# One ScalarE side operation instead of two at the end of each of the first twenty units

## Chip, cores and metric

The kernel runs on one core of one Trainium2 chip. The metric is the device time of one execution in microseconds (us). It is given as the median of several runs, and one further execution was recorded by the hardware profiler. Engines are named as in the profile: PE (TensorE matmul), PEld (its weight loads), DVE (VectorE), ACT (ScalarE), POOL (GpSimd), SP (SyncE, which here issues every DMA).

## Reference

Three layers run one after the other, all in float32.

```
# 1. mLSTM, 4 batches x 8 heads, 768 steps, head size 40
m_new = max(f + m, i);  fs = exp(f + m - m_new);  is_ = exp(i - m_new)
C = fs*C + is_ * outer(v_t, k_t);  n = fs*n + is_*k_t
y_t = sigmoid(o_gate_t) * (C q_t) / max(|n.q_t|, 1)
# 2. soft mixture of experts, 3072 tokens x 320, 8 experts x 4 slots, FF 1024
logits = x @ phi;  d = softmax over tokens;  c = softmax over slots
out = c @ [ relu((d.T @ x)_e @ w1[e]) @ w2[e] for e ]
# 3. MLP: relu(x @ w_in)**2 @ w_out,   320 -> 2048 -> 320
```

## Kernel before

**The units.** The first layer is cut into 11 groups of up to three heads and six chunks of 128 steps: 66 units (u0 to u65). Each turn of the loop over `units` (L881) issues the parts of several units. It makes the gate broadcast of unit i+3 (`e_mb`, L440), the scores of unit i+2 (`e_st`, L471), the state update of unit i (`e_u`, L499, then `e_uc`, L518 or L515, then the masking `e_mask` on POOL, L534), the product of scores and gate weights of unit i+2 (`e_pm`, L483 on DVE), the exponentials of unit i+3 (`e_exp`, L454, three on ACT), and their triangle mask (`e_sel`, L461 on POOL). Every second unit multiplies the weights with the values (`e_av`, L559) and the queries with the state before (`e_inter`, L544).

**The side work.** Everything else of this stage stands in a list `fillers` of generators, each of which yields the tag of its next step: "A" for a step on ACT, "n" and "N" for DVE, "D" for DVE, "G" and "g" for POOL, "P" for PE, "W" for a point to wait for or a DMA to issue. `advance(tag, limit)` runs up to `limit` steps whose tag is asked for; `filler(seq)` calls it for each letter of `seq`. At the end of each unit `filler(END, ...)` runs with END = "PADNngG". The "A" steps are the gate's tanh (`sigm`, L660, 12 in all), the absolute values in `fin` (L607), copies and exponentials of the expert layer (`moe_tokens`), and the conversions of `w_in` (`win_all`, which calls `narrow`).

**The conversion of w_in.** `win_all` loads ten pieces of `w_in` (128x1024 words, L168) in turn into the two halves of the tile `stage`, and converts each in four steps: L140 and L144 on ACT, L148 and L152 on DVE. A piece's load waits until the conversion that read its half is done. The generator is always sorted to the end of `fillers`. Its "n" steps run only where the unit has run no other "N" or "D" step. When all ten are converted, "win" stands in `done`, and only then the first two halves of the expert layer's second weight (w2 of f = 0) are loaded into the same tile:

```
        if "win" in done and w2s:
            ld_w2(*w2s.pop(0))
...
    while fillers:
        advance("W")
        filler("PNADngG")
    while w2s:
        ld_w2(*w2s.pop(0))
```

The first two lines stand in the loop over units, the others behind it. Behind them follow, on the same SP queue, the w2 halves of f = 3 into `par0` (`ld_w2`, L123; in the kernel before they are part of one run of three), `wo0` (the first four row blocks of `w_out`, L991), two half-size loads of `w_out` (`xTw`, `x`), w2 of f = 4 (`w2x`) and w2 of f = 5 to 7 (six halves into `ring`, over the first weights, which L1113 must have read). SP issues in program order, so a DMA that waits holds all behind it.

**The expert layer's end.** `ffn_up` (L1113) multiplies the slots with w1; `relu` (L1118 on ACT) needs `rt128` (L1137 on DVE). Ahead of L1137 on DVE stand L148 and L152 of `wo_narrow(0)`, which convert `wo0`, behind L140 and L144 of the same on ACT. `ffn_tr` (L1164) transposes the result, and `ffn_down(f)` (L1183, f = 0 to 7) multiplies it with w2 of f, two halves each. The last layer (L1226 on) follows.

Of the kernel before, what the change touches and what calls it, by code (L numbers as in the profile page):

```python
# [18 lines left out]
PL, DL, SG = 2, 2, 2  # L19
# [4 lines left out]
LI, LT = 42, "NADG"  # L24
# [18 lines left out]
def kernel(  # L43
# [20 lines left out]
    D = DM // H  # L64
# [746 lines left out]
    def split(t):  # L811
        return (t, set()) if not isinstance(t, tuple) else t
# [6 lines left out]
    def advance(tag, limit=9):  # L819
        n = limit  # L820
        for f in list(fillers):
            while limit and f[1] in tag and f[3] <= done:
                limit -= 1
                t = next(f[0], None)
                if t is None:
                    fillers.remove(f)
                    done.add(f[2])
                    break
                f[1], f[3] = split(t)
        return n - limit  # L830
# [9 lines left out]
    def filler(seq, late=False, early=False):  # L840
        nn = 0
        for ch in seq:
            if ch == "n":
                if not nn:
                    advance("n", DL)
                continue
            k = advance(ch, {"P": PL, "A": 2, "D": 2 - early, "G": 2 - early}.get(ch, 1) + (late and ch in LT))
            nn += k if ch in "ND" else 0

    w2o = [(f, p) for f in range(FF // 128) for p in range(2)]  # L850
# [28 lines left out]
    late = []  # L879
    xq = [(b, c) for b in range(1, B) for c in range(0, NC, 2)]  # L880
    for i, (g, c) in enumerate(units):  # L881
# [41 lines left out]
        if MID:  # L923
            filler(MID)
# [36 lines left out]
        if i + 3 < NU:  # L961
# [3 lines left out]
            elif g3 > 1 and c3 % 3 == 0:  # L965
                e_wv(g3, c3, c3 + 3)
        filler(END, i >= LI, i < 20)
    xf = xb[B - 2].rearrange("p c d -> p (c d)")
    hsb = xf[:, 0:FF]
# [8 lines left out]
# [3 lines that stand above are left out]
# [525 lines left out]
```

## Time and profile before

| | us |
|---|---|
| median of 3 runs | 390.84 (390.78 to 390.98) |
| the profiled execution, its own time | 390.83 |
| its span, first to last instruction | 389.1 |
| PE busy | 379.6 |
| DVE busy | 264.5 |
| ACT busy | 253.4 |
| POOL busy | 102.4 |

The span is what the trace's times count in, from 0 to 389.1; 1.7 us of the execution's own time lie outside it. The units run from about 10 to 153 us, the end of the expert layer from there to about 182, the last layer from there to the end. A start time in a timeline row is that of the first instruction of the row; where it has "x24", 24 instructions are merged. An idle time in brackets stands ahead of the row's first instruction, with what ended it.

### The profile page before, as it was taken

What the parts mean: (1) busy time and instruction counts of PE and PEld (TensorE: products, weight loads), DVE (VectorE), ACT (ScalarE), POOL (GpSimd) and SP (SyncE); (2) the same over time, 40 slices, a digit from 0 to 9 for tenths busy, and PEclk for the clock granted to TensorE, in tenths of its full rate; (3) what the DMA queues carried; (4) which work ended last, traced back from release to release, by engine and by line L of the source; (5) the groups of instructions that cost most, each with busy time, mean ns of one, the idle gap of its engine ahead of it and who ended that gap; (6) DMA issues with size and microseconds to landing.
All of it is one profiled execution on the core that took longest, in us unless ns stands there. A gap on an engine that the chain in (4) does not pass through costs nothing.

```text
span 389.1 us, 9201 instructions
## 1 busy us (share of the span) xinstructions
PE 379.6 (98%) x3438; PEld 335.1 (86%) x3438; DVE 264.5 (68%) x614; ACT 253.4 (65%) x579; POOL 102.4 (26%) x208
## 2 busy tenths in 40 slices
PE   8899899999999999999999999999999999999996
PEld 6799798798988885435799999999999999999996
DVE  7978788777878777537699956556555655655551
ACT  7797754768566653344697976676676667667662
POOL 4665867775667645000000000000000000000000
PEclk9999999999999999999999999999999999999999
DMA  6886987898879896999000010020010001002001
GB/s 194 257 297 208 289 275 232 254 332 286 260 255 338 286 320 201 361 374 374 3 2 1 3 67 2 0 69 0 3 60 10 0 2 67 3 0 69 1 2 67
DMA packets 19541, 56.62 MB, mean 146 GB/s; under 512 B 2481, under 2 KB 7561, under 8 KB 19113
## 3 DMA queue, kind: packets, MB, share of 16 engines
q1 hardware_dynamic: 19497, 56.04, 42.6%
q8 instruction: 27, 0.44, 0.5%
q14 instruction: 17, 0.14, 0.1%
HBM read 52.10 MB, written 3.93 MB: 144 GB/s over the span
## 4 chain that ended last, share of the span: by engine, by line
PE 84%; ACT 5%; DVE 4%; DMA 2%; issue 2%; POOL 1%; SPq 0%; DVEq 0%; ACTq 0%; POOLq 0%
PE ps_mb L1404 17%; PE ps_st L1404 16%; PE ps_st L471 9%; PE ps_lt L1404 9%; PE ps_o L559 5%; PE ps_o L544 4%; PE ps_o L1327 4%; PE ps_mb L499 3%; PE ps_st L1183 2%; PE ps_mb L440 2%; ACT w L454 2%; PE ps_m L1327 2%; PE ps_lt L683 2%; PE ps_m L677 2%; DMA par<-in_q_t_dram 1%
## 5 line engine op out<-in xcount | busy, mean ns | idle before, releaser
L1350 DVE CAST hi<-ring 128x512 fp32r<-128x512 f32 x93 | 39.7, 427 | 59.1 <-ACT ring L1349 49.7
L454 ACT ACTIVATE w<-ps_mb,qt 128x128 f32<-128x128 f32 x192 | 56.7, 371 | 29.6 <-DVE cu L518 23.4
L1351 DVE TENSOR_TENSOR lo<-ring,hi 128x512 fp32r<-128x512 f32 x96 | 66.5, 693 | 10.1 <-PE ps_o L1327 0.5
L1332 ACT ACTIVATE ring<-ps_o 128x512 f32<-128x512 f32 x65 | 38.9, 598 | 35.0 <-PE ps_o L1327 35.0
L1349 ACT ACTIVATE ring<-ring 128x512 f32<-128x512 f32 x93 | 58.8, 632 | 3.0
L471 PE MATMUL ps_st<-par 120*128 120x128 f32 (+1 forms) x384 | 56.9, 284 | 0.4 <-DMA par<-in_q_t_dram 0.4
L1404 PE MATMUL ps_mb<-wohlh,hi 128*128 128x320 f32 x160 | 49.6, 311 | 0.0
L1404 PE MATMUL ps_mb<-wohlh,lo 128*128 128x320 f32 x160 | 49.5, 310 | 0.0
L1404 PE MATMUL ps_mb<-wohll,hi 128*128 128x320 f32 x160 | 49.3, 309 | 0.0
L471 PEld LDWEIGHTS ps_st<-par 120*128 120x128 f32 (+1 forms) x384 | 47.9, 191 | 0.8 <-DVE dec L415 0.5
L461 POOL TENSOR_SCALAR_AFFINE_SELECT w<-w 128x384 f32<-128x384 f32 (+1 forms) x66 | 37.3, 567 | 38.1 <-ACT w L454 37.2
L1404 PE MATMUL ps_st<-wohlh,hi 128*128 128x320 f32 x144 | 44.8, 311 | 0.0
L483 DVE TENSOR_TENSOR p<-ps_st,w 128x384 f32<-128x384 f32 (+1 forms) x66 | 35.7, 540 | 13.4 <-POOL w L461 7.0
L1404 PE MATMUL ps_st<-wohll,hi 128*128 128x320 f32 x144 | 44.7, 310 | 0.0
L1404 PE MATMUL ps_st<-wohlh,lo 128*128 128x320 f32 x144 | 44.7, 310 | 0.0
L1404 PEld LDWEIGHTS ps_mb<-wohll,hi 128*128 128x128 f32 x160 | 30.1, 188 | 1.3
L1332 ACT ACTIVATE ring<-ps_m 128x512 f32<-128x512 f32 x31 | 18.5, 598 | 18.4 <-PE ps_m L1327 18.4
L1404 PEld LDWEIGHTS ps_mb<-wohlh,hi 128*128 128x128 f32 x160 | 30.0, 188 | 0.0
L1404 PEld LDWEIGHTS ps_mb<-wohlh,lo 128*128 128x128 f32 x160 | 30.0, 188 | 0.0
L559 PE MATMUL ps_o<-par,p 128*64 128x41 f32 x768 | 29.0, 232 | 0.0
L1404 PEld LDWEIGHTS ps_st<-wohll,hi 128*128 128x128 f32 x144 | 27.1, 188 | 1.9 <-issue 0.6
L559 PEld LDWEIGHTS ps_o<-par,p 128*64 128x64 f32 x768 | 25.1, 137 | 4.0 <-issue 0.2
(277 smaller groups left out, 777.8 us busy)
## 6 DMA issues: line engine op xcount, KB each, us to landing
ring<-in_w_dram SPq DMA_DIRECT2D x22, 640.0 KB
stage<-in_w_in_dram SPq DMA_DIRECT2D x10, 512.0 KB
par<-in_w_dram SPq DMA_DIRECT2D x6, 640.0 KB
out_dram<-ring SPq DMA_DIRECT2D x24, 160.0 KB
par<-in_v_s_dram SPq DMA_DIRECT2D x9, 369.0 KB
par<-in_k_s_dram SPq DMA_DIRECT2D x9, 360.0 KB
x<-in_o_gate_dram SPq DMA_DIRECT2D x9, 320.0 KB
par<-in_k_t_dram SPq DMA_DIRECT2D x23, 120.0 KB
```

Of the source, the lines that this page charges most:

```text
L454: nc.scalar.activation(w[:, j, :], mb[:, 128 * j : 128 * j + 128], AF.Exp, bias=qt3[:, c, h0 + j : h0 + j + 1])
L461: nc.gpsimd.affine_select(out=w, in_=w, pattern=[[0, nh], [1, 128]], compare_op=ALU.is_ge, fill=0.0, base=0, channel_multiplier=-1)
L471: nc.tensor.matmul(st[:, 128 * j : 128 * j + 128], lhsT=kbd[g % 2][0:nd, j, ts_], rhs=qin[g][0:nd, ts_], start=True, stop=True,)
L483: nc.vector.tensor_tensor(out=p, in0=sts.pop((g, c))[:, 0 : nh * 128].rearrange("p (n t) -> p n t", n=nh), in1=ws.pop((g, c)), op=ALU.mult,)
L544: nc.tensor.matmul(pos[g, c // 2][:, o0 : o0 + nv], lhsT=qin[g][0:nd, 128 * c : 128 * c + 128], rhs=cbds[g, c - 1][0:nd], start=True, stop ...
L559: nc.tensor.matmul(po[t0 : t0 + 64, o0 : o0 + DV], lhsT=p[:, j, t0 : t0 + 64], rhs=vin[g][:, c, j, :], start=True, stop=True,)
L1327: nc.tensor.matmul(t, lhsT=gst[n][:, 128 * k : 128 * k + 128], rhs=cst[tg], start=True, stop=True)
L1332: nc.scalar.activation(r, t, AF.Relu)
L1349: nc.scalar.activation(r, r, AF.Square)
L1350: nc.vector.tensor_copy(hi, r)
L1351: eng.tensor_tensor(out=lo, in0=r, in1=hi.bitcast(F32), op=ALU.subtract)
L1404: nc.tensor.matmul(acc[u][:, 0:DM], lhsT=l_[:, 128 * u : 128 * u + 128], rhs=wohl[r_, f // 8][:, f % 8, :], start=(f == 0 and a == 0), sto ...
```

## Change

At the end of a unit the letter "A" ran up to two steps on ACT. Now it runs up to two only from the twentieth unit on; until then up to one, as "D" and "G" already did (`early` is true for i < 20).

```diff
-            k = advance(ch, {"P": PL, "A": 2, "D": 2 - early, "G": 2 - early}.get(ch, 1) + (late and ch in LT))
+            k = advance(ch, {"P": PL, "A": 2 - early, "D": 2 - early, "G": 2 - early}.get(ch, 1) + (late and ch in LT))
```

What that does to the order is seen on three engines. The number of instructions on each is the same, PE and POOL keep their order, and from u17 to u54 the conversions stand where they stood, two pieces later in count.

On ACT, at u12 to u16 (L660 the tanh, L454 the units' exponentials, L607 the absolute values, L140 and L144 the conversion of `w_in`), the kernel before has:

```order
L454 ACTIVATE w<-ps_mb,qt_109 128x128 x3
L660 ACTIVATE x<-x 128x640
L454 ACTIVATE w<-ps_mb,qt_109 128x128 x3
L607 ACTIVATE rc<-ring 128x18
L140 ACTIVATE wi<-stage 128x512
L454 ACTIVATE w<-ps_mb,qt_109 128x128 x3
L144 ACTIVATE stage<-stage 128x512
L454 ACTIVATE w<-ps_mb,qt_109 128x128 x3
L607 ACTIVATE rc<-ring 128x18
L454 ACTIVATE w<-ps_mb,qt_109 128x128 x3
```

The changed kernel has there:

```order
L454 ACTIVATE w<-ps_mb,qt_109 128x128 x3
L660 ACTIVATE x<-x 128x640
L454 ACTIVATE w<-ps_mb,qt_109 128x128 x3
L607 ACTIVATE rc<-ring 128x18
L454 ACTIVATE w<-ps_mb,qt_109 128x128 x3
L144 ACTIVATE stage<-stage 128x512
L454 ACTIVATE w<-ps_mb,qt_109 128x128 x3
L607 ACTIVATE rc<-ring 128x18
L454 ACTIVATE w<-ps_mb,qt_109 128x128 x3
```

The L140 of u14 is gone, and the L144 of u15 belongs to the first piece instead of the third. In u8 to u12 the kernel before has two more L140 and two L144, the changed one has a single L140 at u10. The two pieces that are done later on ACT stand at u56 and u57, and at u62 and u64.

On DVE, behind the last unit (L652 and L653 end the first layer, L1034 opens the last token block's softmax), the difference is:

```order
 L652 RECIPROCAL rcl<-rcl 128x4
 L653 TENSOR_TENSOR x<-x,rcl 128x2x80
+L148 SCALAR_TENSOR_TENSOR stage<-stage 128x512
+L152 SCALAR_TENSOR_TENSOR wi<-wi,stage 128x512
 L1034 TENSOR_REDUCE nmx<-ps_lt 96x1
 L1036 TENSOR_SCALAR mx_114<-nmx 96x1
```

The tenth piece's conversion ends there; before, it stood at u54, and the ninth's, now at u60, stood at u50.

On SP, at the end of the units, the difference is:

```order
 L116 DMA ring<-in_w_dram 128x1280
-L123 DMA par_70<-in_w_dram 128x1280 x3
+L123 DMA par_70<-in_w_dram 128x1280
+L123 DMA stage<-in_w_dram 128x1280 x2
+L123 DMA par_70<-in_w_dram 128x1280 x2
 L991 DMA wo_2724<-in_w_out_dram 128x2560
 L991 DMA xTw<-in_w_out_dram 128x1280
```

The two w2 loads into `stage` moved here, ahead of two of the three loads into `par0` and of `wo0`. Before, they were issued in the units around u54. Two loads of `w_in` pieces (L168) moved from u12 and u15 to u50 and u54.

## Rows read from the trace of the kernel before

**Rows 1.** Busy time of each engine by stretch: length, engines, PEclk, DMA share, GB/s.

```profile
30.00:40.00 10.00, 10.00 (x141) 9.45 (x141) 7.66 (x18) 8.21 (x23) 5.39 (x11) 1.00 0.67 197
```

**Rows 2.** Timeline of PE in u9 to u15.

```profile
30.94 0.89 PE L471 MATMUL ps_st<-par 120*128 120x128 f32 x6
...
34.40 0.89 PE L471 MATMUL ps_st<-par 120*128 120x128 f32 x6
...
42.34 0.48 PE L544 MATMUL ps_o<-cbd,par 120*128 120x123 f32 x2 [1.21 <-POOL cbd L534]
```

**Rows 3.** Timeline of ACT and POOL ahead of that wait.

```profile
38.14 0.66 ACT L140 ACTIVATE wi<-stage 128x512 f32<-128x512 f32 x1
...
38.71 0.86 ACT L454 ACTIVATE w<-ps_mb,qt 128x128 f32<-128x128 f32 x3
...
39.65 0.53 POOL L461 TENSOR_SCALAR_AFFINE_SELECT w<-w 128x384 f32<-128x384 f32 x1 [1.02 <-ACT w L454]
...
41.45 0.84 POOL L534 TENSOR_TENSOR cbd<-cu,hm 120x123 f32<-120x123 f32 x1
```

**Rows 4.** Instructions that touch `stage`: ns min/median/max, first and last start.

```profile
L140 ACT ACTIVATE wi<-stage x10: 662/679/723, 26.2 to 120.9; 128x512 f32<-128x512 f32 x10
L144 ACT ACTIVATE stage<-stage x10: 662/702/728, 28.1 to 122.3; 128x512 int32<-128x512 uint16 x10
L148 DVE SCALAR_TENSOR_TENSOR stage<-stage x10: 672/810/1129, 29.3 to 126.5; 128x512 int32<-128x512 int32 x10
L152 DVE SCALAR_TENSOR_TENSOR wi<-wi,stage x10: 691/888/1178, 30.0 to 127.2; 128x512 int32<-128x512 int32 x10
```

**Rows 5.** Timeline of DVE behind the last unit.

```profile
154.80 0.33 DVE L653 TENSOR_TENSOR x<-x,rcl 128x160 f32<-128x160 f32 x1
156.90 0.42 DVE L1034 TENSOR_REDUCE nmx<-ps_lt 96x1 f32<-96x256 f32 x1 [1.77 <-PE ps_lt L1021]
```

**Rows 6.** Timeline of SP: the issue of loads.

```profile
127.25 0.35 SPq L123 DMA_DIRECT2D stage<-in_w_dram  x1
...
149.31 4.02 SPq L123 DMA_DIRECT2D par<-in_w_dram  x3
155.29 0.33 SPq L991 DMA_DIRECT2D wo<-in_w_out_dram  x1
```

**Rows 7.** DMA issues from 145 to 190 us: count and KB each.

```profile
ring<-in_w_dram SPq DMA_DIRECT2D x6, 640.0 KB
...
wo<-in_w_out_dram SPq DMA_DIRECT2D x1, 1280.0 KB
```

**Rows 8.** Busy time by stretch at the end of the expert layer.

```profile
150.00:156.00 6.00, 5.80 (x60) 3.60 (x56) 3.96 (x17) 1.72 (x5) 2.07 (x6) 1.00 0.93 309
158.00:182.00 24.00, 23.92 (x257) 10.24 (x258) 14.15 (x41) 10.53 (x19) 1.90 (x2) 1.00 1.00 389
168.00:182.00 14.00, 14.00 (x177) 5.80 (x166) 9.03 (x19) 7.65 (x14) 0.00 (x0) 1.00 1.01 409
```

**Rows 9.** Timeline of ACT and DVE around the first `relu`.

```profile
160.88 0.78 ACT L140 ACTIVATE par<-wo 128x640 f32<-128x640 f32 x1 [0.31 <-DMA wo<-in_w_out_dram]
...
167.39 0.69 ACT L1118 ACTIVATE x<-ps_st,rt 128x512 f32<-128x512 f32 x1 [5.06 <-DVE rt L1137]
167.98 0.80 ACT L140 ACTIVATE par<-wo 128x640 f32<-128x640 f32 x1
...
167.20 0.16 DVE L1137 COPY rt<-ps_m 128x1 f32<-128x1 f32 x1 [1.07 <-PE ps_m L1136]
...
171.13 0.35 DVE L1049 COPY en<-ps_o 128x192 f32<-128x192 f32 x1
```

**Rows 10.** Timeline of PE: the first transposes, the last halves of w2, what follows.

```profile
170.12 0.66 PE L1164 MATMUL ps_mb<-ident,x 128*128 128x128 f32 x4
...
178.56 3.41 PE L1183 MATMUL ps_st<-ring 128*32 128x320 f32 x48
181.90 0.66 PE L1226 MATMUL ps_m<-ident,chl 128*128 128x128 f32 x4
```

## Prediction

> **What bounds the kernel now.** I read the engine totals first: PE is busy for 379.6 of the 389.1 us, so time is won only where PE really waits, and lost wherever a change makes it wait. The busy time by stretch then says where the change could help: from 30 to 40 us ACT is busy for 8.21 of 10 us [rows 1], the densest it gets beside the tanh steps, so that taking ACT work out looks promising there. But PE is busy for all 10. A busy PE can be an illusion of modelled ends, so the next view is PE's timeline by start times. Two units repeat one pattern, and the scores of every second unit start at 30.94 and 34.40 [rows 2], 3.46 us apart, with no idle time marked between them. PE is the pace there, and ACT's density is hidden under it. The first wait of PE behind this stretch is at 42.34: 1.21 us for the masked state from POOL [rows 2]. That is the one place where less ACT work can give something back.
>
> The third view is the end of the units and of the expert layer, since the change moves work there. From 158 to 182 us the DMA engines are busy for 100% of the time at a mean of 389 GB/s, and from 168 to 182 at 409 GB/s [rows 8]. PE is busy too (23.92 of 24 us), so today loads and PE just keep step. A load that comes later into this stretch pushes all behind it.
>
> **The change part by part.**
>
> *Early.* Four ACT steps (two L140, two L144) and four DVE steps (two L148, two L152) leave u8 to u15. By the medians [rows 4] that is 2 x (0.68 + 0.70) = 2.8 us of ACT and 2 x (0.81 + 0.89) = 3.4 us of DVE. Up to about 41 us they are worth nothing: PE sets the pace over them (3.46 us for two units). The cover is gone at 42.34. The chain into that wait runs: L140 at 38.14 holds the exponentials to 38.71, POOL's mask L461 at 39.65 had waited 1.02 us for them, and two more POOL operations stand between it and the state's masking L534 at 41.45 [rows 3], which PE waits for. The changed order has no L140 there, so the exponentials and all behind them come 38.71 - 38.14 = 0.57 us earlier. L148 and L152 of u15 stay where they are, only with another piece. Bounds: nothing (if POOL is held by something else) to the whole wait of 1.21 us. I take -0.6, since the removed L140 is directly ahead of the chain and the rest of POOL's queue does not change.
>
> *Middle.* From u17 to u54 each step stands where it stood. 0.
>
> *Late.* Two pieces are converted in u56 to u64 and behind the units. Two pairs of ACT steps go in, 2.8 us by the same medians, and one DVE pair at u60, 1.7 us. ACT and DVE have idle time between units there, and what waits for the exponentials (POOL, then L483 on DVE, one unit later) has a unit's time. Bounds: 0 to 1.0 us, the latter if one of the pairs falls fully on the way; I take +0.1. The last DVE pair stands between L653, which ends at 154.80 + 0.33 = 155.13, and L1034, which had been idle for 1.77 us until PE at 156.90 [rows 5]. The shortest L148 and L152 take 0.67 + 0.69 = 1.4 us, the medians 1.7 [rows 4]: both fit under that wait, 0. If the cover failed, the longest (1.13 + 1.18) would cost 0.5.
>
> *The w2 loads into `stage`.* They were issued from 127.25 on [rows 6] and had landed long before use. Now the first waits for the last L148, so SP issues it at about 155.13 + 0.7 = 155.9. SP is in program order, so two of the `par0` loads (issued from 149.31 on before) and `wo0` (155.29 before) come behind it [rows 6]. The queue between 153 and 156 us runs dry, and from 155.9 on it has to bring: stage 2, par0 2, `wo0` 1280 KB which is 2, the two half loads of w_out 1 each, w2x 2, and ring 6 halves of 640 KB [rows 7]; all halves of w2 are the same shape. That is 16 x 655,360 bytes = 10.49 MB up to the last half of f = 7, and 6 halves = 3.93 MB up to `wo0`.
>
> How fast: 409 GB/s, as in the stretch where the queue is never short [rows 8]; the 389 of the longer stretch has two short dips in it and is the lower bound. How long until a fresh queue moves: from 149.31 to 156 it brought 6 x 309 = 1.85 MB [rows 8], which at 409 takes 4.5 us, so the start-up is at most about 2 us (part of it is SP's own spacing); at least 0. I take 2, the only row that has it. Then `wo0` lands at 155.9 + 2.0 + 9.6 = 167.5 (160.88 before, [rows 9]) and the last half of w2 at 155.9 + 2.0 + 25.6 = 183.5.
>
> What waits: L140 of `wo0` on ACT, and through L144, L148, L152 the L1137 on DVE. The second such conversion shows the length of that chain: L140 at 167.98, and the next DVE instruction behind its L152 (L1049) at 171.13, so 3.15 us [rows 9]. L1137 comes at 167.5 + 3.15 = 170.65 instead of 167.20, the relu L1118 starts 0.19 later (as 167.39 to 167.20) and takes 0.69 [rows 9]. PE's first transposes L1164 then start at about 171.5 instead of 170.12 [rows 10]: +1.4. All of f = 0 to 7 moves by that. The 48 instructions of f = 5 to 7 take from 178.56 to 181.90 [rows 10], so the last half (8 of them) starts at 181.34, and 1.4 later at 182.7. But it lands at 183.5: another 0.8 us. The end of the expert layer moves by 1.4 + 0.8 = 2.2 us, and since nothing behind it waits for a fixed time, the kernel's end does too. Bounds: with no start-up, `wo0` at 165.5 is still in time and the last half at 181.5 costs 0.2; with 389 GB/s and 2 us the last half lands at 184.9: 3.5.
>
> A rule of the Trainium skill bears on the rate: "DMA: Bandwidth & Descriptors", section "Bandwidth", says that for loads from HBM the HBM share of a core, about 358 GB/s, is what binds. By that figure the last half would land (an estimate) at 187.2 and the tail would cost 5.9 us. The 409 GB/s held over 14 us in [rows 8] contradict it for this run, and the measured figure decides.
>
> *Sum.* Against the profiled execution's own 390.83 us (span 389.1 and 1.7 around it; the median of the runs, 390.84, is the same): 390.83 - 0.6 + 0.1 + 2.2 = 392.5 us.
>
> **The rivals.** A change under 0.2% (0.8 us) cannot be told from none.
> - *The loads are hidden anyway* (no change). If the queue starts at once and runs at 409, the tail costs 0.2: 390.83 - 0.6 + 0.1 + 0.2 = 390.5. For it: no PE wait on a load shows in this stretch today, so some slack exists (the last half, by the same sum, had landed at 160.88 + 10 x 0.655 / 0.409 = 176.9 against 181.34). Against it: 1.31 MB more in a queue that is 100% busy take 3.2 us, and the dry time ahead takes the rest.
> - *The early relief wins* (faster). The whole wait at 42.34 goes, -1.2, and the tail costs the 0.2 above: 389.8. It decides from the point where the tail costs less than about 0.4, that is if `wo0` lands before 166. For it: ACT's removed step is right ahead of the chain. Against it: the DVE pair of u15, beside which POOL's L534 took 0.84 us [rows 3], is still there, and the tail has to be nearly free.
> - *Both late costs come* (slower still). 389 GB/s and a late pair on the way, with no early gain: 390.83 + 1.0 + 3.5 = 395.3. For it: the mean over the longer stretch. Against it: its dips come where the queue ran short, which a backlog does not.
> - That the change does nothing is excluded: the order of ACT, DVE and SP changes as shown.
>
> **How the numbers follow.** The forecast, a tail of 1 to 3.5 us and a small early gain, gets 0.67; hidden loads 0.17; the early relief 0.08; both late costs 0.08. The predicted time is 392.5; the likeliest case's own range is 391.7 to 394.0. The range for 8 in 10 reaches from the hidden loads to the upper bound of the tail without the early gain, 390.4 to 394.3, and leaves out the faster case and the slowest. Chances: faster 0.08, the same 0.17, slower 0.75.
>
> **What would show it right or wrong.** Right: SP issues the two w2 loads into `stage` at about 155 to 156 (shifted by the early gain) instead of 127; almost no DMA between 153 and 156; ACT's L140 of `wo0` waits for its DMA until 167; L1118 about 3.5 us later; PE's L1164 waits; and the halves of f = 6 and 7 have PE waits on the `ring` loads. The stretch u9 to u14 keeps its 3.46 us per two units, and the wait at 42.34 is halved. Wrong: a queue that brings `wo0` by 165, or a pace of units that drops under 3.46 us without the conversions, or new PE waits at u56 to u62, which I cost at 0.1.

## Result and profile after

The changed kernel takes 393.98 us in the median (393.58 to 395.18, 4 runs) against 390.91 us of the kernel before beside it: a ratio of 1.0084 (95% interval 1.0071 to 1.0096), 3.1 us slower. The profiled execution took 393.82 us with a span of 392.1, that is 3.0 us more than before in both. The direction was as forecast, and so was the chain of waits at the end; of the two terms that make the sum, the early gain was 1.55 us instead of 0.6, by a second path, and the loss at the end 4.5 us instead of 2.2.

**Early.** PE's timeline of the changed kernel at the place of [rows 2] (start, duration, line, form; idle time in brackets):

```profile
30.88 0.89 PE L471 MATMUL ps_st<-par 120*128 120x128 f32 x6
...
34.34 0.89 PE L471 MATMUL ps_st<-par 120*128 120x128 f32 x6
...
40.15 0.89 PE L471 MATMUL ps_st<-par 120*128 120x128 f32 x6
40.92 0.48 PE L544 MATMUL ps_o<-cbd,par 120*128 120x123 f32 x2
```

The pace of 3.46 us for two units has not changed, and the wait of 1.21 us ahead of L544 is gone altogether. What stands ahead of it on DVE, ACT and POOL, in the same profile:

```profile
35.91 0.40 DVE L588 TENSOR_TENSOR ring<-ps_o,tmp 128x246 f32<-128x246 f32 x1
...
36.35 0.23 ACT L607 ACTIVATE rc<-ring 128x18 f32<-128x18 f32 x1 [0.20 <-DVE ring L588]
37.27 0.88 ACT L454 ACTIVATE w<-ps_mb,qt 128x128 f32<-128x128 f32 x3 [0.69 <-DVE cbd L515]
...
38.23 0.53 POOL L461 TENSOR_SCALAR_AFFINE_SELECT w<-w 128x384 f32<-128x384 f32 x1 [1.21 <-ACT w L454]
...
40.03 0.84 POOL L534 TENSOR_TENSOR cbd<-cu,hm 120x123 f32<-120x123 f32 x1
```

Against [rows 3] the exponentials come 1.44 us earlier (37.27 against 38.71) and L534 1.42 us earlier. ACT has even become idle ahead of them: the step L140 that was removed had 0.57 us, so something else moved too. It is L607, which in the kernel before started at 38.00 and had itself waited for DVE's L588; and L588 stood behind the pair L148, L152 of u12, which the change also removed. In the kernel before:

```profile
35.42 0.84 DVE L148 SCALAR_TENSOR_TENSOR stage<-stage 128x512 int32<-128x512 int32 x1
36.29 0.89 DVE L152 SCALAR_TENSOR_TENSOR wi<-wi,stage 128x512 int32<-128x512 int32 x1
...
37.57 0.40 DVE L588 TENSOR_TENSOR ring<-ps_o,tmp 128x246 f32<-128x246 f32 x1
...
38.00 0.23 ACT L607 ACTIVATE rc<-ring 128x18 f32<-128x18 f32 x1 [0.63 <-DVE ring L588]
```

With the pair gone, L588 comes 1.66 us earlier and L607 1.65. By u23 the units run 1.55 us earlier, and they keep that to the last one: the late conversions cost nothing.

**Late.** SP's issue of loads (compare [rows 6]), with the time that issuing took as the second column:

```profile
147.76 0.33 SPq L123 DMA_DIRECT2D par<-in_w_dram  x1
154.24 1.02 SPq L123 DMA_DIRECT2D stage<-in_w_dram  x2
155.35 1.07 SPq L123 DMA_DIRECT2D par<-in_w_dram  x2
156.52 0.50 SPq L991 DMA_DIRECT2D wo<-in_w_out_dram  x1
```

Then ACT, DVE and PE around the first `relu` (compare [rows 9, 10]):

```profile
167.41 0.82 ACT L140 ACTIVATE par<-wo 128x640 f32<-128x640 f32 x1 [8.40 <-DMA wo<-in_w_out_dram]
...
170.73 0.69 ACT L1118 ACTIVATE x<-ps_st,rt 128x512 f32<-128x512 f32 x1 [1.82 <-DVE rt L1137]
...
155.35 0.42 DVE L1034 TENSOR_REDUCE nmx<-ps_lt 96x1 f32<-96x256 f32 x1 [0.45 <-PE ps_lt L1021]
...
171.47 0.89 PE L1164 MATMUL ps_mb<-ident,x 128*128 128x128 f32 x4 [2.84 <-ACT x L1118]
172.29 3.32 PE L1113 MATMUL ps_o<-ring,x 128*32 128x512 f32 x16
175.44 1.25 PE L1183 MATMUL ps_st<-stage,ring 128*32 128x320 f32 x16
...
181.54 3.41 PE L1183 MATMUL ps_st<-ring 128*32 128x320 f32 x48
184.89 0.66 PE L1226 MATMUL ps_m<-ident,chl 128*128 128x128 f32 x4
```

SP waits for the last conversion from 148.1 to 154.24; `wo0` is released only 13.1 us behind the first load into `stage`; L1118 and PE wait for it, PE by 2.84 us. Last, the busy time by stretch (length, engines, PEclk, DMA share, GB/s):

```profile
152.00:154.00 2.00, 2.00 (x16) 1.23 (x14) 1.90 (x8) 0.26 (x2) 0.98 (x2) 1.00 0.01 4
...
156.00:168.00 12.00, 11.62 (x101) 4.95 (x104) 3.52 (x20) 1.76 (x6) 1.90 (x2) 1.00 1.00 404
168.00:182.00 14.00, 11.16 (x120) 4.44 (x116) 7.86 (x15) 7.96 (x15) 0.00 (x0) 0.88 1.02 416
...
171.80:175.20 3.40, 3.40 (x20) 0.96 (x21) 2.30 (x5) 1.12 (x3) 0.00 (x0) 0.50 1.01 411
```

The queue is empty from 152 to 154, then full at 404 and 416 GB/s, so the rate was the 409 of the forecast to within 2%. Behind PE's wait its granted clock is at 0.50, the lower of its two levels (1.2 instead of 2.4 GHz), for 3.4 us. From L653, the end of the units, to L1226, the first matmuls of the last layer, it takes 31.64 us instead of 27.10: 4.54 more, less the 1.55 won, is the 3.0 of the span.

### The profile page after: what moved, and what is told of

Read it like the earlier page. It is cut to its first block, busy times and chain, and to the rows that moved or that the text cites. A ratio compares the mean times of both kernels' runs of the same rounds, so it can differ in the third digit from the quotient of the medians.

```text
span 392.1 us, 9201 instructions
## 1 busy us (share of the span) xinstructions
PE 380.5 (97%) x3438; PEld 335.1 (85%) x3438; DVE 264.7 (68%) x614; ACT 253.2 (65%) x579; POOL 102.8 (26%) x208
## 4 chain that ended last, share of the span: by engine, by line
PE 84%; ACT 5%; DVE 4%; DMA 3%; issue 1%; POOL 1%; SPq 0%; ACTq 0%; DVEq 0%; POOLq 0%
PE ps_mb L1404 17%; PE ps_st L1404 16%; PE ps_st L471 10%; PE ps_lt L1404 8%; PE ps_o L559 6%; PE ps_o L544 5%; PE ps_o L1327 4%; PE ps_mb L499 3%; DMA wo<-in_w_out_dram 3%; PE ps_mb L440 2%; PE ps_st L1183 2%; PE ps_m L1327 2%; PE ps_lt L683 2%; PE ps_m L677 2%; PE ps_m L725 1%
## 5 line engine op out<-in xcount | busy, mean ns | idle before, releaser
L454 ACT ACTIVATE w<-ps_mb,qt 128x128 f32<-128x128 f32 x192 | 56.7, 370 | 29.8 <-DVE cu L518 22.5
L471 PE MATMUL ps_st<-par 120*128 120x128 f32 (+1 forms) x384 | 56.9, 284 | 0.8 <-DMA par<-in_q_t_dram 0.6
L471 PEld LDWEIGHTS ps_st<-par 120*128 120x128 f32 (+1 forms) x384 | 47.9, 191 | 1.2 <-DVE ring L367 0.8
```

Of the source, the lines that this page charges most:

```text
L454: nc.scalar.activation(w[:, j, :], mb[:, 128 * j : 128 * j + 128], AF.Exp, bias=qt3[:, c, h0 + j : h0 + j + 1])
L471: nc.tensor.matmul(st[:, 128 * j : 128 * j + 128], lhsT=kbd[g % 2][0:nd, j, ts_], rhs=qin[g][0:nd, ts_], start=True, stop=True,)
```

## Experiments

Beside each ratio stands its 95% interval against the kernel before, measured on the same chip.

**The tail alone.** Kernel before, with the last w_in piece's two DVE steps held behind the units; nothing moves early.

```diff
-            yield from narrow(..., t, apart=True)
+            for tag in narrow(..., t, apart=True):
+                yield "Z" if tag == "n" and n == len(wins) - 1 else tag
...
-        advance("W")
+        advance("WZ")
```

> The kernel before, where only the two DVE steps of the last w_in piece are held back behind the units. The early part is as before, the end as in the changed kernel. Theory: the whole loss without the early gain: 390.9 + 4.5 = 395.4, with the wait at L1164 and the half clock. Rival (a part of the loss comes from the ACT and DVE steps put into u56 to u64, which stay out here): less than 393.

395.02 us (394.50 to 395.64), ratio 1.0105 (1.0090 to 1.0121). PE in its profiled run, where the clock stayed at 1.00:

```profile
172.68 0.66 PE L1165 MATMUL ps_mb<-ident,x 128*128 128x128 f32 x4 [2.63 <-ACT x L1119]
...
184.39 1.27 PE L1184 MATMUL ps_st<-ring 128*32 128x320 f32 x12 [0.41 <-DMA ring<-in_w_dram]
185.59 0.66 PE L1227 MATMUL ps_m<-ident,chl 128*128 128x128 f32 x4
```

So one conversion that ends late is enough for the whole loss: L1226's counterpart comes 3.7 us later than in [rows 10], through both waits that the forecast named, the one for `wo0` and the one for the last half of w2.

**Late loads that nothing holds.** Kernel before, without the two lines in the loop that issue the w2 loads into `stage` (the conversions end as early as ever, so behind the units the loads wait for nothing).

```diff
-        if "win" in done and w2s:
-            ld_w2(*w2s.pop(0))
```

> The kernel before, where the two w2 loads into stage stand at the same late place on SP as in the changed kernel, but the conversions of w_in keep their old places, so that the loads need not wait for the last conversion. Theory (the loss is the queue standing dry until the last conversion is done): the loads fill the dry time from 149 to 153 us, wo0 lands about 1.7 us later than before (160.9 to 162.6), which is in time for DVE: 390.8 to 391.4. Rival (the later bytes alone): 393 to 394.

390.82 us, ratio 0.9997 (0.9988 to 1.0007). The 1.31 MB go out at 149.73 instead of 127, right between the `par0` loads, and cost nothing. `wo0` comes 3.4 us later by these bytes (its last part is in at 164.15 us instead of 160.77), and that is only just hidden: the first `relu` starts 0.25 us later (167.64 instead of 167.39), and PE's L1164 does not move (its counterpart starts at 170.10). So the bytes ahead of `wo0` alone cost nothing. It is the empty queue that comes on top of them in the changed kernel that costs: a load that waits on SP holds all behind it.

**`wo0` first.** Changed kernel, the two loads into `stage` moved behind that of `wo0`.

```diff
-    while w2s:
-        ld_w2(*w2s.pop(0))
...
     load_wo(wo0, 0, 4)
+    while w2s:
+        ld_w2(*w2s.pop(0))
```

> The changed kernel, with the two w2 loads into stage issued on SP behind wo0 instead of ahead of two par0 loads and wo0. All bytes stay the same. Theory (wo0 comes late, so the first relu is late, so PE waits and its clock falls): wo0 lands again before DVE needs it, the PE wait at L1164 (2.84 us) and the half clock go, and the early gain of 1.55 us is kept: about 389.3 us, faster than both kernels. Rival (the 1.31 MB more in a full queue are the cost, whatever their order): PE waits as long, only later, on the stage or ring halves: 393 to 394.

390.06 us (389.46 to 390.42), ratio 0.9975 (0.9966 to 0.9984): faster than both kernels.

```profile
159.48 0.79 ACT L140 ACTIVATE par<-wo 128x640 f32<-128x640 f32 x1 [0.53 <-DMA wo<-in_w_out_dram]
...
168.51 0.66 PE L1164 MATMUL ps_mb<-ident,x 128*128 128x128 f32 x4
...
176.94 3.72 PE L1183 MATMUL ps_st<-ring 128*32 128x320 f32 x48
```

The early gain stays, PE waits neither for L1118 nor at half clock, and of the tail only 0.3 us are left in the last w2 halves (3.72 instead of 3.41 us). These rows are from the fastest of its ten runs (389.46 us); the median is 0.6 us longer, which no row here explains. The cause of the loss is settled by this: the order behind one late wait on SP.

**Full clock.** Changed kernel with 24 warm-up matmuls in PE's wait.

```diff
     ffn_up(1, range(0, 3))
+    warm(24)
     ffn_tr(0)
```

> The changed kernel with 24 small matmuls into an unused bank ahead of the first L1164, so that PE works through most of its 2.84 us wait for the first relu. They compute nothing that is used. Theory (half clock from 171.8 to 175.2 us follows from PE's idling and costs 1.6 us): the clock stays at full, L1164 to the first L1183 takes 2.3 instead of 4.0 us: 392.3. Rival (the stretch is slow because of the loads, not the clock): no change, 393.9.

393.56 us (393.23 to 393.77), ratio 1.0066 (1.0053 to 1.0080). The clock is at 1.00 throughout and L1183 starts 2.32 us behind L1164 instead of 3.97; but the 1.6 us are nearly all lost again:

```profile
171.53 0.66 PE L1164 MATMUL ps_mb<-ident,x 128*128 128x128 f32 x4
...
179.96 2.86 PE L1184 MATMUL ps_st<-ring 128*32 128x320 f32 x36
183.63 1.27 PE L1184 MATMUL ps_st<-ring 128*32 128x320 f32 x12 [0.80 <-DMA ring<-in_w_dram]
184.83 0.66 PE L1227 MATMUL ps_m<-ident,chl 128*128 128x128 f32 x4
```

The last half of w2 is a second floor at almost the same height as the half clock. My expectation had left it out, though the forecast had it.

**Which early step counts.** Kernel before, with the limit of one ACT step for two units of the loop only: units 8 and 9 (shown), in a second run 11 and 12. Both leave the conversions done in time, so the tail is that of before.

```diff
-            k = advance(ch, {"P": PL, "A": 2, "D": ...
+            k = advance(ch, {"P": PL, "A": 2 - one, "D": ...
...
-        filler(END, i >= LI, i < 20)
+        filler(END, i >= LI, i < 20, i in (8, 9))
```

> The limit of one step holds for the loop's units 8 and 9 alone. That takes the DVE pair L148/L152 out from behind the units' L581 near 35.4 us, but leaves one conversion (L144 in place of L140) ahead of the exponentials of 38.71 us. The tenth piece still ends inside the units, so nothing of the loads behind them waits for it. Theory (the DVE pair held L588, that held L607 on ACT, that held the exponentials; the ACT conversion itself fits into ACT's wait once L607 is early): the full early gain, 1.5 us, and no loss at the end, 389.3 us. Rival (as forecast: the ACT conversion ahead of the exponentials is what held them): no gain, 390.8 us.

> The limit of one step holds for the loop's units 11 and 12 alone. That takes the conversion L140 out from ahead of the exponentials of 38.71 us, and leaves the DVE pair near 35.4 us. Theory (the DVE pair held L588 and L607): L607 still comes at 38.0 us, so only the 0.57 us of L140 are won, as forecast: 390.3 us. Rival (the conversion on ACT was the whole cause): 1.5 us won, 389.3 us.

Units 8 and 9: 389.64 us, ratio 0.9969 (0.9957 to 0.9981). Units 11 and 12: 389.80 us, ratio 0.9972 (0.9960 to 0.9983). For units 8 and 9, where L144 still stands ahead of the exponentials:

```profile
36.81 0.73 ACT L144 ACTIVATE stage<-stage 128x512 int32<-128x512 uint16 x1
37.38 0.93 ACT L454 ACTIVATE w<-ps_mb,qt 128x128 f32<-128x128 f32 x3
...
40.19 0.84 POOL L534 TENSOR_TENSOR cbd<-cu,hm 120x123 f32<-120x123 f32 x1
```

For units 11 and 12, with the DVE pair of u12 in its place:

```profile
38.13 0.23 ACT L607 ACTIVATE rc<-ring 128x18 f32<-128x18 f32 x1 [0.64 <-DVE ring L588]
38.38 0.88 ACT L454 ACTIVATE w<-ps_mb,qt 128x128 f32<-128x128 f32 x3
...
41.14 0.39 POOL L534 TENSOR_TENSOR cbd<-cu,hm 120x123 f32<-120x123 f32 x1
...
41.59 0.48 PE L544 MATMUL ps_o<-cbd,par 120*128 120x123 f32 x2 [0.33 <-POOL cbd L534]
```

The theory holds for the first: without the DVE pair the exponentials are 1.3 us earlier although an ACT conversion is still ahead of them, and that alone is worth 1.2 us. For the second, L607 stays at 38.1 as the theory said, and the exponentials follow it by 0.25 us instead of 0.71, so the removed ACT step gives 0.5 us as the forecast had it. But the run won 1.0 instead of the 0.6 expected, because this edit also takes away the later DVE pair (41.00 in the kernel before), and L534, then alone, takes 0.39 us instead of 0.84. The two gains don't add up (1.55 together in the changed kernel, where L534 keeps its 0.84), since each eats into one wait.

**Why `wo0` came 1.5 us later than summed.** My first theory was that loads issued behind it moved bytes first. Two runs on it. In one the loads of `xTw`, `x` and `w2x` are moved behind the first of `ring`; in the other (with the warm-up) the two w_out loads of L1200 and L1249 are held back until f = 4 is done, by a small load into the tile that f = 4 reads.

```diff
-    load_wo(xTw[:, 0 : SLOT // 2], 6, 2)
...
-    load_wo(x3.rearrange("p c d -> p (c d)")[:, 0 : SLOT // 2], 4, 2)
-    for n in (6, 7):
-        ld_w2(w2p[n], *w2o[2 + n])
...
-    for n in range(6):
+    for n in range(1):
         ld_w2(ring_half(2 * (n % 3) + n // 3), *w2o[10 + n])
+    load_wo(x3.rearrange("p c d -> p (c d)")[:, 0 : SLOT // 2], 4, 2)
+    for n in (6, 7):
+        ld_w2(w2p[n], *w2o[2 + n])
+    load_wo(xTw[:, 0 : SLOT // 2], 6, 2)
+    for n in range(1, 6):
+        ld_w2(ring_half(2 * (n % 3) + n // 3), *w2o[10 + n])
```

```diff
-    load_wo(stage, 8, 4)
...
-    load_wo(par[1][:, 0:SLOT], 12, 4)
...
     for f in range(4, 8):
         ffn_down(f)
+        if f == 4:
+            nc.sync.dma_start(out=w2x[:, 0:64], in_=w2[0, :, 0, 0:64])
+            load_wo(stage, 8, 4)
+            load_wo(par[1][:, 0:SLOT], 12, 4)
```

> The changed kernel with the three half loads and w2x that are issued between wo0 and the ring moved behind the first ring load, which waits until about 163.6 us. Ahead of that only the five loads up to wo0 are on the queue (3.93 MB). Theory (loads that are issued later move bytes before an earlier one has landed; 0.8 MB did so): wo0 lands at about 165.4 instead of 167.3 us, L1164 starts about 1.9 us earlier, at 169.6, the clock does not fall, and the last half of w2 still comes at about 183.5 behind a wait, as with the warm-up: 393.5 us. Rival (loads land in the order of their issue, and the rate to wo0 was simply lower): wo0 still at 167.3, the whole time 394.0 us or more.

> The changed kernel with the 24 warm-up matmuls, and the two w_out loads into stage and par (2.6 MB, issued at 175.2 and 177.0 us with the warm-up) held back on SP until f = 4 has read w2x, by a load of 32 KB into it. Theory (bytes of those later loads passed the last w2 halves; in the order of issue these would have been there at about 181): PE's wait of 0.80 us on ring is gone, 392.7 us. Rival (the last half lands when it does by the rate alone): the wait stays, 393.5 us.

The first gave 394.31 us, ratio 1.0093 (1.0078 to 1.0108), the second 393.50 us, 1.0070 (1.0058 to 1.0082). ACT in the first, PE in the second:

```profile
167.76 0.82 ACT L140 ACTIVATE par<-wo 128x640 f32<-128x640 f32 x1 [8.50 <-DMA wo<-in_w_out_dram]
```

```profile
183.83 1.27 PE L1184 MATMUL ps_st<-ring 128*32 128x320 f32 x12 [0.58 <-DMA ring<-in_w_dram]
```

`wo0` alone on the queue is still 13.2 us behind the first load (154.51 to 167.66), and the last half still keeps PE waiting. The theory falls. What the trace then showed is the landing of each load in parts: it holds 16 landing events for one load, and the waiting engine goes on with the last. For some loads (us; the issue of the first load into `stage` in brackets):

```
kernel, load                              first   median  15th    last
before, wo0                               160.26  160.52  160.72  160.77
before, xTw (the load behind wo0)         161.98  162.14  162.64  164.08
after (154.24), second half into stage    159.26  159.51  159.85  160.15
after, next load (par0)                   160.85  161.09  161.70  162.64
after, wo0                                165.56  165.81  166.37  167.31
after, last half of w2                    181.36  181.62  183.10  183.25
```

The loads follow each other in the order of issue, one half of w2 every 1.58 us. But from the third load on one part is about 1 us behind the rest, and stays behind in every load up to the last. In the last three halves a second part is late as well, which is why the 15th stands at 183.10 in the last row. In just that stretch the DMA view of the changed kernel (160 to 162 us; packets, MB, share of 16 engines) has another queue in it:

```profile
q1 hardware_dynamic: 171, 0.80, 99.4%
q8 instruction: 1, 0.02, 3.0%
```

3.0% of 16 engines in 2 us is one engine for 0.97 us: a 16 KB packet of instructions, at 160.20. In the kernel before it came at 161.95, behind `wo0`. That gives a theory that can be tried: shift the packet.

**The instruction packet shifted.** Changed kernel; the 36 warm-up matmuls at its very start are replaced by 84 shorter ones, so that all of PE's later instructions stand 96 further on (48 matmuls, 48 weight loads). The control has 52, so 32 further on. The third run has the 84 with `wo0` first.

```diff
-                warm(int(ch[1:]))
+                if ch == "~36":
+                    for _ in range(36 + 48):
+                        nc.tensor.matmul(dum[:, 0:80], lhsT=zb[:, 0:128], rhs=zb[:, 0:80], ...)
+                else:
+                    warm(int(ch[1:]))
```

> The changed kernel with the 36 warm-up matmuls at its very start replaced by 84 shorter ones (80 columns instead of 256), so that PE's later instructions stand 48 matmuls and 48 weight loads later in its program. Theory (the 16 KB packet of the instruction queue at 160.2 us belongs to PE's program and holds up one of the 16 shares of every load behind it by its own 1 us, until the queue runs empty): the packet comes some 6 us earlier in the same program, into the stretch near 153.5 us where no load is on the queue; wo0 is then released 11.6 to 11.9 us behind the first load into stage instead of 13.1, L1164 starts 1.3 us earlier, and its wait falls from 2.8 to about 1.5 us. The next packet then falls near 169 us, so the last w2 half still lands late: 393.5 us. Rival (the lag of the last share has another cause): wo0 still 13.1 us behind, 394 us.

> The same with 52 short matmuls instead of 84, so 16 more than before: the control for the shorter matmuls. Theory: the instruction packet comes some 2 us earlier, near 158 us, still behind the first loads of the queue and ahead of wo0, so wo0 is still released about 13.1 us behind the first load into stage: 394 us. Rival (the shorter matmuls at the start themselves change the end): the same as with 84.

> wo0 ahead of the two loads into stage, with the 84 short matmuls at the start. Theory: nothing waits for wo0 there, and the lag of the last share at the last w2 half comes from the packet near 169 us instead of that at 160 us: the same 390.0 us within 0.4. Rival: the shorter warm-up costs PE clock or time at the start, more than 390.5 us.

With 84: 393.50 us (393.19 to 394.23), ratio 1.0065 (1.0052 to 1.0078). With 52: 395.68 us (394.68 to 397.00), 1.0125 (1.0105 to 1.0144). With `wo0` first and 84: 389.76 us, 0.9975 (0.9964 to 0.9985), as expected, so the shorter matmuls at the start cost nothing by themselves there. The DMA view of 152 to 154 us with 84, and then of 160 to 162 with 52:

```profile
q8 instruction: 1, 0.02, 4.1%
q1 hardware_dynamic: 13, 0.01, 1.5%
q14 instruction: 1, 0.01, 1.4%
```

```profile
q1 hardware_dynamic: 184, 0.81, 100.1%
q8 instruction: 1, 0.02, 3.0%
```

```
kernel, load                              first   median  15th    last
84 (155.19), wo0                          166.50  166.75  167.02  167.18
84, load behind wo0                       168.09  168.35  168.76  169.82
84, last half of w2                       182.35  182.59  183.97  184.12
52 (155.30), wo0                          166.66  167.00  167.28  168.47
```

PE with 84, then with 52:

```profile
171.38 0.65 PE L1168 MATMUL ps_mb<-ident,x 128*128 128x128 f32 x4 [1.79 <-ACT x L1122]
...
184.16 1.27 PE L1187 MATMUL ps_st<-ring 128*32 128x320 f32 x12 [0.97 <-DMA ring<-in_w_dram]
```

```profile
172.63 0.99 PE L1168 MATMUL ps_mb<-ident,x 128*128 128x128 f32 x4 [2.93 <-ACT x L1122]
```

Both profiled runs are late from the first units on: the first load into `stage` goes out at 155.19 us with 84 and at 155.30 with 52, against 154.24 in the changed kernel. So times are compared from that load on.

With the packet in the empty queue (152.46), `wo0` is whole 11.99 us behind the first load and PE waits 1.79 us; with the packet at 161.22 it takes 13.17 and PE waits 2.93. The next packet of the run with 84 comes at 167.67, and from the load behind `wo0` on one part is late again, to the last half. This is shown: behind an instruction packet that falls into a full queue, one part of every later load is late, until the queue runs empty; a packet in the empty queue leaves no such lag. That the packet and the late part share one of the 16 DMA engines is inferred from the time and the size, since the trace does not name the engine.

That it is PE's own program that this packet belongs to fits too. The queue brings 27 such packets in the changed kernel for PE's 3,438 matmuls and as many weight loads, one for every 255 of them, and 96 more moved it from 5.96 us behind the first load to 2.73 us ahead of it. But 32 more did not move it by the 2 us that I expected: it came 5.92 us behind the first load. So the run with 52 is a control for the shorter matmuls, and by what rule the packet comes stays open.

With 52 the clock behind PE's wait fell as in the changed kernel (a mean of 0.73 over 170 to 176 us against 0.72), so this is not what makes that run the longest. Its profiled execution (394.95 us) is 1.1 us over that of the changed kernel, as much as it is late at the first load, and its granted clock was also at 0.50 from 9.0 to 15.7 us. Why its other executions take up to 397.00 us stays open.

## Why the prediction was right or wrong

Two terms of the sum failed, with opposite signs: the early gain, put at -0.6, measured -1.55, and the tail, put at +2.2, measured +4.5.

- **PE sets the pace up to 41 us, and the first wait is the place to win.** Right, as the rows above show.
- **The early gain, -0.6.** Mis-sized: -1.55. The step that failed is "Up to about 41 us they are worth nothing". PE's pace did hide the DVE pair of u12 from PE, but not from ACT: L588, behind it, released L607, and L607 stood ahead of the exponentials of the priced chain. The upper bound of 1.21 fell too: L544 of that wait came 1.42 us earlier (40.92 against 42.34). From the L471 ahead of it, it takes 0.77 us instead of 2.09, so the idle time that the profile marks was not all that PE lost there. The pair alone is worth 1.2 us, the ACT step itself 0.5, as forecast. The kernel before showed it: L607 waited there 0.63 us for DVE's L588, one row above the L140 of [rows 3].
- **Middle 0, late conversions +0.1, the pair behind L653 0.** Right: the shift stays at 1.55 us from u23 to the last unit, and L1034 still waits for PE (0.45 us).
- **The queue: order of issue, 2 us of start-up, 409 GB/s.** Right for the median part of each load. From the measured issue at 154.24 the forecast's sum gives 165.8 for `wo0` and 181.8 for the last half; the medians of the parts are 165.81 and 181.62. The two rates that bounded it (389 and 409) were not what was uncertain. The 358 GB/s that the prediction takes from the Trainium skill, "DMA: Bandwidth & Descriptors", section "Bandwidth", is by the same section what each core gets with both cores of an HBM domain loading; for one core alone it lists 425 GB/s at 16 MB, and the 404 and 416 GB/s of this one-core kernel are nearer to that.
- **What waits: +1.4 for `relu`.** The chain was right, the size not; the term that failed is the landing of `wo0`, summed from bytes and rate. `wo0` counts only when its last part is in, 1.5 us behind the sum, so L1164 came 2.9 us later against the end of the units, not 1.4. In [rows 9] this lag could not be seen, since the packet came behind `wo0` there. The Trainium skill, "DMA: Bandwidth & Descriptors", section "Why a DMA increments its semaphore by 16 and not by 1", says that the 16 engines of one DMA finish independently and that only the full count means that all data landed; the landing events agree. "Runtime: NRT & Kernel Launch", section "Instruction fetch mechanics", has instructions refilled in blocks of 16 KiB at a cost that is mostly hidden; the size agrees, the cost was not hidden here.
- **The last half, +0.8.** The wait exists (0.80 us at full clock, 0.41 in the tail alone). In the changed kernel itself the half clock hides it. The slack was mis-sized: the rival of hidden loads puts the last half at 176.9 in the kernel before, with 4.4 us in hand, but its median part came at 177.96 and its last at 180.16, 0.3 us ahead of the first matmul that waits for it (180.46). Worked out on its rows: by the forecast's sum the last half lands at 181.8 and its 8 instructions end 0.6 later, 182.4, against 181.90 - 1.55 = 180.35 without a tail: 2.1, the forecast's 2.2. Then 12 instructions wait for the half, not 8, and take 1.2 (rows with the warm-up): +0.6. Its last part is at 183.25: +1.4. The half clock comes out later than that floor, 184.89 against 184.5: +0.4. Together 4.5.
- **The half clock** was not in the forecast. It cost the profiled run 0.4 us, and the spread of the four runs goes with the clock: 393.58 us at a mean granted clock of 1.000, 395.18 at 0.990. Where the runs without a profile lost their clock is not shown.
- **The range.** The upper bound of 3.5 for the tail came from a rate, and no rate could have given the lag of one part. The time still fell inside the range because the two errors have opposite signs, and that is luck.

## What to carry to other kernels

When a wait at the end of a chain is to be priced, go up the chain past the first removed step: what releases the instruction ahead of it may be on the list of removed steps too, on an engine that looked covered. A load that waits in program order on the issuing queue costs more than its own bytes, since the queue stands empty ahead of everything behind it: put the loads that are needed first ahead of the one that may wait (here 3.9 us, the difference between the changed kernel and the one with `wo0` first). A load from a full queue is there when the slowest of its 16 parts is: in the changed kernel 1.4 to 1.5 us over bytes by rate, and in the run with `wo0` alone 3.2 us behind the median part (185.33 against 182.12 for the last half).

## What was not expected of the hardware

- One instruction packet of 16 KB held one DMA engine for about 1 us (0.97 at 160.20), and 23 us later, in the last half of w2, one part was still late. The spread of the parts, first to last, was 1.8 us at `wo0` and 1.7 eleven us later, so nothing was caught up in the full queue. A second packet made another part late in the changed kernel (at 176.73; the 15th part was 0.5 us behind the median before it and 1.5 behind it after), and in the run with `wo0` alone (at 177.21) the spread grew from 2.4 to 3.6 us.
- PE's granted clock fell to 0.50 for 3.4 us behind a wait of 2.84 us in the changed kernel, and likewise behind 2.93 us with 52 matmuls. It did not behind 2.94 us in the run with `wo0` alone, nor behind 2.63 us in the tail alone, nor behind 1.79 us. So the wait by itself does not settle it; what else does stays open.
- POOL's L534 takes 0.84 us where it starts 0.45 us after DVE's L148 has started (41.45 in the kernel before), and 0.39 on the same 120x123 elements where it starts 0.10 us ahead of an L148 (35.32) or has none beside it. It is not the overlap but the order: in the units of the kernel before, each of the 13 POOL operations that start inside an L148 or L152 ends 0.15 to 0.67 us behind that instruction. Why is not shown.
